# Queries and keys loaded as rows of four tokens, a new attention order, and slot inputs divided while they are copied

## The chip, the cores and the metric

The kernel runs on one core of a Trainium2 chip. A core has TensorE for matrix products (PE in the rows), VectorE (DVE), ScalarE (ACT), GpSimd (POOL) and SyncE (SP), which here only issues transfers; 16 DMA engines move data between the chip's memory (HBM) and the core's on-chip memory (SBUF). Matrix products land in PSUM, eight banks of 512 float32 in each of 128 partitions. Each engine works through its own list of instructions in order and waits on semaphores.

The metric is the device time of one execution in microseconds (us), the median of several.

## The reference, cut to what matters

```
q, k, v: 4 batches x 12 heads x 448 tokens x 64        (float32)
scores = q @ k.T / 8, causal mask; attn = exp(scores - rowmax)
attn   = attn / (attn.sum + 1e-9);  x = attn @ v       -> 1792 x 768

logits = x @ phi                                       # 1792 x 32 slots
d = exp(logits - logits.max over tokens);  d /= d.sum over tokens + 1e-9
slot_input = d.T @ x                                   # 32 x 768
slot_out[e] = relu(slot_input[e] @ w1[e]) @ w2[e]      # 8 experts of 4 slots
c = exp(logits - logits.max over slots);   c /= c.sum + 1e-9
x = c @ slot_out                                       # 1792 x 768

out = (sigmoid(x @ w_gate) * (x @ w_val)) @ w_out      # 768 -> 1536 -> 768
```

## The kernel before, in words

The kernel has three stages, and each starts on what the one before leaves.

**Attention with the slot logits.** A pair is two heads of one batch (24 pairs, number i), a group is four heads (12 groups, number g, two pairs each). For a group, `load_qk` and `load_v` bring q, k and v into `qkbuf[g % 2]` and `vbuf[g % 2]`: 128 tokens on the partitions, four chunks of tokens (the last has 64), the heads side by side; `load` issues one transfer a chunk for all four heads. Group 0 is loaded by `load_first` in two halves, heads 0 and 1 first, the keys of that half issued by ACT and all else by SP. For the split of q and k into float16 halves the group's mean square is needed first: `first_squares` and `squares_1` (groups 0 and 1, on DVE and ACT), `squares` and `add_up` (later groups, on POOL), then `spread` (a small product, psq) and `scales` (four small DVE instructions, the last ones qkp, qks and sc).

A pair then runs: `st_T` transposes its q and its k on TensorE (four transposes each into one psT bank), `st_hi` on ACT writes the scaled float16 value, `st_lo` on DVE what is left of it (both into tile qT), `score` forms the scores by three products of halves (psS; one set for each 128 queries, sets 0 to 2 and the last 64 as set 3), `st_m` masks and takes the row minimum of the negated scores on DVE, `st_e` takes the exponent on ACT into P, `st_P` transposes P on TensorE (psP), `st_C` copies it to PT on ACT or DVE, `st_V` multiplies by v (psV), `st_xu` copies, `st_Xa` transposes back (psX), `st_xn` divides by the row sums. For two pairs at once `st_Y` forms the logits (psY), `st_U` transposes them (psU). Each batch ends with the `tl_` functions: column maximum, exponents (en), and `tl_A`/`tl_a`, which gather the slots' unnormalised input over tokens in acc.

**The end of attention.** Only 32 token classes by 32 slots have been kept apart, so `fo` puts the four parts of the running maximum and sum together in eight steps on PE, DVE and ACT: `fw` is a factor for each row, `zw` the weighted sum, `fo(6)` adds the sums up (psm3), `fo(7)` takes the reciprocal `rz` and makes `fww` from fold, fw and rz. `to_slots` multiplies acc by `fww` (p4, in the rows psm with 32 columns), a copy brings it to `slotT`, and `first_inner` forms the first expert's first product (psh). Between these stand products of ones that nothing reads (`keep_warm`, psf).

**The order of the attention.** All of this is put in order by `Plan.play`: every step is an `op` with an engine and a cost, what it depends on, the buffers it takes and the time it is due; play builds the instruction lists by earliest start and due time. The table `SHIFT` and the constants `ASLACK`, `AMARGIN`, `AWAIT` move due times, so they alone decide the order of otherwise equal work. Loads are steps of an engine "D", which is SP's queue. Ten weight transfers of 1.5 MB (`load_w`) are spread over this stage.

**The experts and the gated unit.** The other expert weights and those of the gated unit follow on SP's queue into buffers that lie where the attention's tiles lay, and into the first ten again; a transfer is issued when the last reader of the buffer is done. TensorE multiplies as they come (psh, so). The gated unit at the end (psg, psv, pso, six column blocks) has a plan of its own, which the change leaves alone.

All instructions of both plans carry the number of one helper line, L218, in the rows.

## Time and profile before

| | |
|---|---|
| median of 3 runs | 528.49 us (527.89 to 530.23) |
| the profiled execution | 528.25 us, its span 526.5 us |
| TensorE busy | 480.0 us (91% of the span) |
| DVE, ACT, POOL busy | 395.3, 332.1, 279.8 us |
| moved by DMA | 101.56 MB; of 87660 packets 68784 under 512 B |
| the chain that ended last | PE 76%, DMA 12%, DVE 7% |

How the rows below are read: a timeline row has the start of the first instruction, the time to the end of the last one, the engine (q behind it means that it issues a transfer; PEld is TensorE's load of weights), the line, the operation, output<-inputs with shapes, the count, and in brackets how long the engine stood idle before it and what ended that. The ends of TensorE's instructions overlap the next one, so the step from one start to the next is the price of a product there, not the length of a row. A row of stretches has its limits, its length, and for each engine the busy time and the count in brackets, then the granted TensorE clock (1.00 is 2.4 GHz, 0.50 is 1.2 GHz), the DMA engines' mean busy share and GB/s. The chain of waits is followed back from the last instruction.

### The profile page before, as it was taken

Reading aid. Unit: us, or ns where it says so; the run is one execution under the profiler, and the core shown is the slowest. Engines: PE = TensorE matmul, PEld = TensorE weight load, DVE = VectorE, ACT = ScalarE, POOL = GpSimd, SP = SyncE. Lnnn points to the kernel's source line nnn. Section 1 sums busy time; section 2 is a strip of 40 time slices with the busy share of each in tenths; the row PEclk is TensorE's granted clock in tenths of the full one; section 3 lists DMA queues with packets and bytes.
Section 4 is the critical chain, followed back from the end, with each engine's and each line's share of the span. In section 5 each row is a group of like instructions: output and inputs, shape, how many; then the busy total and the mean of one; then the engine's idle time right before and its main releaser. Section 6 shows DMA issues by size and latency. Waiting matters only on the chain.

```text
span 526.5 us, 12472 instructions
## 1 busy us (share of the span) xinstructions
PE 480.0 (91%) x4649; PEld 295.9 (56%) x4649; DVE 395.3 (75%) x980; ACT 332.1 (63%) x740; POOL 279.8 (53%) x376
## 2 busy tenths in 40 slices
PE   5799999999999999999835579999999999989997
PEld 3467767767667676555412235555555555555553
DVE  4688989889889986521064069899999998986874
ACT  3688887889788886111190059878777588474420
POOL 4078868778768712000000013359899798867630
PEclk9899999999999999999979899999999999999999
DMA  5756646665767357799999992452063060210144
GB/s 133 170 167 196 198 106 187 139 194 178 211 162 196 126 183 273 287 423 418 408 408 425 411 395 93 164 195 90 33 241 121 0 240 2 71 51 1 60 175 184
DMA packets 87660, 101.56 MB, mean 193 GB/s; under 512 B 68784, under 2 KB 69040, under 8 KB 85552
## 3 DMA queue, kind: packets, MB, share of 16 engines
q1 hardware_dynamic: 86640, 100.55, 55.9%
q8 instruction: 36, 0.59, 0.4%
q10 hardware_dynamic: 960, 0.23, 0.2%
q14 instruction: 24, 0.20, 0.1%
HBM read 95.26 MB, written 5.51 MB: 191 GB/s over the span
## 4 chain that ended last, share of the span: by engine, by line
PE 76%; DMA 12%; DVE 7%; SPq 2%; issue 2%; ACT 1%; DVEq 0%; ACTq 0%
PE pso L218 27%; PE psP L218 9%; PE psV L218 9%; PE psS L218 8%; DMA w<-in_moe_w_dram 6%; DMA w<-in_moe_w_gate_dram 5%; PE psg L218 4%; PE psT L218 4%; PE so L1011 3%; PE psY L218 2%; PE psX L218 2%; DVE w L218 2%; SPq L218 2%; PE psh L998 2%; DMA k<-in_k_dram 1%
## 5 line engine op out<-in xcount | busy, mean ns | idle before, releaser
L218 POOL TENSOR_TENSOR hlo<-hs,hhi 128x448 f16<-128x448 f32 x48 | 69.8, 1469 | 124.7 <-ACT hhi L218 116.3
L218 PEld LDWEIGHTS <-hhi 128*128 128x128 f16 (+1 forms) x768 | 65.1, 101 | 56.0 <-issue 16.6
L218 PE MATMUL pso<-wh,hhi 128*128 128x384 f16 (+1 forms) x384 | 84.4, 328 | 4.9 <-DVE oacc L218 3.1
L218 ACT ACTIVATE P<-psS,nm 128x256 f32<-128x256 f32 (+3 forms) x168 | 82.3, 505 | 10.4 <-DVE nm L218 9.3
L218 POOL TENSOR_TENSOR oacc<-oacc,ev 128x384 f32<-128x384 f32 x56 | 76.3, 1382 | 15.9 <-ACT ev L218 15.9
L218 PE MATMUL pso<-wh,hlo 128*128 128x384 f16 (+1 forms) x384 | 82.3, 326 | 0.0
L218 PE MATMUL pso<-wl,hhi 128*128 128x384 f16 (+1 forms) x384 | 82.2, 326 | 0.0
L218 DVE CUSTOM_DVE_ANT_0 psS<-psS,cmaskq,sc 128x128 f32<-128x128 f32 (+2 forms) x144 | 62.7, 488 | 3.5 <-PE psS L218 3.3
L218 DVE SCALAR_TENSOR_TENSOR w<-w 128x1536 int32<-128x1536 int32 x30 | 62.0, 2069 | 2.4 <-ACT w L218 2.3
L218 DVE SCALAR_TENSOR_TENSOR oacc<-pso,osc,oacc 128x384 f32<-128x384 f32 x84 | 49.8, 610 | 14.0 <-PE pso L218 12.9
L218 PE MATMUL psP<-ident,P 128*128 128x128 f32 x384 | 57.6, 285 | 0.5 <-ACT P L218 0.5
L218 PE MATMUL psS<-qT,qT 64*64 64x256 f16 (+3 forms) x1008 | 50.3, 298 | 5.3 <-ACT qT L218 1.9
L218 POOL TENSOR_TENSOR sq<-sq 128x512 bf16<-128x512 bf16 (+1 forms) x80 | 51.2, 640 | 6.0
L218 ACT COPY PT<-psP 128x512 f32<-128x512 f32 x86 | 47.0, 589 | 7.0 <-PE psV L218 4.3
L218 ACT ACTIVATE w<-w 128x1536 int32<-128x1536 uint16 (+1 forms) x30 | 49.1, 1649 | 3.5 <-DMA w<-in_moe_w_gate_dram 3.5
L218 ACT ACTIVATE ev<-pso,osc 128x384 f32<-128x384 f32 x56 | 32.5, 582 | 27.7 <-PE pso L218 19.8
L218 PEld LDWEIGHTS psP<-ident,P 128*128 128x128 f32 x384 | 43.0, 144 | 7.9 <-issue 3.1
L218 PE MATMUL psV<-PT,v 128*64 128x448 f32 (+3 forms) x384 | 46.8, 385 | 0.0
L218 PEld LDWEIGHTS <-hlo 128*128 128x128 f16 (+1 forms) x384 | 33.8, 101 | 20.8
L301 DVE TENSOR_SCALAR hm<-psh,emask 128x256 f32<-128x256 f32 x8 | 5.3, 667 | 46.3 <-PE psh L998 43.8
L218 PEld LDWEIGHTS <-qT 64*64 64x64 f16 x1008 | 28.3, 109 | 20.9 <-issue 7.8
L218 PEld LDWEIGHTS psV<-PT,v 128*64 128x64 f32 x384 | 25.5, 136 | 22.8 <-issue 14.6
(298 smaller groups left out, 839.1 us busy)
## 6 DMA issues: line engine op xcount, KB each, us to landing
w<-in_moe_w_dram SPq DMA_DIRECT2D x32, 1536.0 KB, 8.4
w<-in_moe_w_out_dram SPq DMA_DIRECT2D x6, 1536.0 KB, 9.8
w<-in_moe_w_val_dram SPq DMA_DIRECT2D x6, 1536.0 KB, 13.4
w<-in_moe_w_gate_dram SPq DMA_DIRECT2D x6, 1536.0 KB, 6.6
out_dram<-oacc SPq DMA_DIRECT2D x13, 384.0 KB, 2.3
v<-in_v_dram SPq DMA_DIRECT2D x36, 128.0 KB, 3.0
q<-in_q_dram SPq DMA_DIRECT2D x33, 128.0 KB, 3.0
k<-in_k_dram SPq DMA_DIRECT2D x33, 128.0 KB, 3.0
```

Of the source, the lines that this page charges most:

```text
L218: x = f(*a, **kw)
L301: nc.vector.tensor_scalar(to.rearrange("s (i q) -> s q i", i=2), ps.rearrange("s (q i) -> s q i", i=2), 0.0, emask[:, e:e + 1], ALU.max, A ...
L998: nc.tensor.matmul(ps[32 * g:32 * g + 32, :], lhsT=slotT[:, kc, :], rhs=w[:, kc % 3, 256 * g:256 * g + 256], start=kc == 0, stop=kc == KC - 1)
L1011: nc.tensor.matmul(so[32 * c:32 * c + 32, :], lhsT=hT[:, i, 32 * g:32 * g + 32], rhs=w[:, f % 4, 256 * c:256 * c + 256], start=e == 0 and ...
```

## The change

**Rows of four tokens.** q and k of a head are read as 112 rows of four consecutive tokens: token 4p + j goes to partition p, place j. One transfer brings one head (112 partitions, four pieces of 64 values). `st_T` makes four transposes of 112 columns in place of 128, with a 112 by 112 identity. PSUM then holds the tokens by j first; `st_hi` and `st_lo` read it with a step of 112 floats (`in_order`) and write qT in token order. The squares and their sums use 112 partitions, those of group 0 go to the tile `sqbuf` in place of the second v buffer, and the four clearings of q and k tails fall away. v is loaded as before. Group 0's first half needs two transfers each of q and k in place of four.

**Division at the copy.** `fo(5)` makes `fww` from fold and fw alone. `fo(6)` forms the sums for all 128 partitions by 32 slots, `fo(7)` takes the reciprocal of that, and `to_slotT` multiplies by it while it copies to `slotT`. `to_slots` depends on `fo(5)` and no longer on `fo(7)`.

**Order.** The costs of loads in the plan are those of issuing them, with the flight as a lag; `SHIFT` and the three constants have new values; the tiles of scales and of the first squares count as buffers (`sg`, `sq`). The products that nothing reads are half as wide (256 columns), 28 in place of 19.

```
-    ASLACK, AMARGIN, AWAIT = 0.635, 1.671, 0.074
+    ASLACK, AMARGIN, AWAIT = 1.317, 1.41, 0.087
...
-    SHIFT = {('A', 0): 7.76, ('A', 1): -7.71, ('C', 0): -17.75, ('C', 1): 76.61, ('C', 2): 23.02, ('C', 3): 22.6,
+    SHIFT = {('A', 0): 8.92, ('A', 1): 24.1, ('C', 0): 11.69, ('C', 1): 67.2, ('C', 2): 31.78, ('C', 3): 30.98, ('S',
...
+        def rows_in(e, t, src):
+            for h in range(src.shape[0]):
+                e.dma_start(out=t[:RP, :, h * D:h * D + D], in_=src[h].rearrange("(p j) d -> p j d", j=RJ))
+
         def load_qk(g, w):
+            b, h0, nh = GRP[g]
             grp.setdefault(g, {"qk": qkbuf[g % 2]})
-            load(qkbuf[g % 2][w], (q, k)[w], g)
+            rows_in(sp, qkbuf[g % 2][w], (q, k)[w][b, h0:h0 + nh])
...
             for w, src in enumerate((q, k)):
-                for j, (s0, n) in enumerate(CH):
-                    (ac if w and not o else sp).dma_start(
-                        out=qkbuf[0][w][:n, j, o * D:(o + 2) * D].rearrange("p (h d) -> p h d", d=D),
-                        in_=src[0, o:o + 2, s0:s0 + n, :].rearrange("h p d -> p h d"))
+                rows_in(ac if w and not o else sp, qkbuf[0][w][:, :, o * D:(o + 2) * D], src[0, o:o + 2])
...
-            for j in range(4):
-                te.transpose(ps[:, 128 * j:128 * j + 128], grp[g]["qk"][w][:, j, o * D:(o + 2) * D], ident)
+            for j in range(RJ):
+                te.transpose(ps[:, RP * j:RP * j + RP], grp[g]["qk"][w][:RP, j, o * D:(o + 2) * D], ident[:RP, :RP])
+
+        def in_order(x):
+            return x.rearrange("p (j c) -> p c j", j=RJ)
+
+        def by_rows(x):
+            return x.rearrange("p (c j) -> p c j", j=RJ)
...
-            ac.activation(out=hi, in_=pr[i]["ps", w][:, :S], func=AF.Copy, scale=scale_of(i)[:, w:w + 1])
+            ac.activation(out=by_rows(hi), in_=in_order(pr[i]["ps", w][:, :S]), func=AF.Copy, scale=scale_of(i)[:, w:w + 1])
...
-            ve.scalar_tensor_tensor(lo, d.pop(("ps", w))[:, :S], scale_of(i)[:, w:w + 1], d["hi", w], ALU.mult, ALU.subtract)
+            ve.scalar_tensor_tensor(by_rows(lo), in_order(d.pop(("ps", w))[:, :S]), scale_of(i)[:, w:w + 1], by_rows(d["hi", w]), ALU.mult, ALU.subtract)
...
-            te.matmul(fin["f"].rearrange("p (a b) -> p a b", a=4), lhsT=ones, rhs=ones.rearrange("p (a b) -> p a b", a=1).to_broadcast([128, 4, 128]),
-                      start=True, stop=True)
+            te.matmul(fin["f"][:, :256].rearrange("p (a b) -> p a b", a=2), lhsT=ones,
+                      rhs=ones.rearrange("p (a b) -> p a b", a=1).to_broadcast([128, 2, 128]), start=True, stop=True)
...
                 ve.tensor_tensor(fin["zw"], zrun, fin["w"], ALU.mult)
+                fw = fin["fw"] = tl_p.tile([128, NS], F32, tag="mrow", name="fww")
+                ve.tensor_scalar(fw, fold, fin["w"], None, ALU.mult)
             elif n == 6:
-                fin["p3"] = psS.tile([128, 1], F32, tag="s", name="psm3")
-                te.matmul(fin["p3"], lhsT=fold4.rearrange("p a s -> p (a s)"), rhs=fin["zw"], start=True, stop=True)
+                fin["p3"] = psS.tile([128, NS], F32, tag="s", name="psm3")
+                te.matmul(fin["p3"], lhsT=fin["zw"].to_broadcast([128, 128]), rhs=fold, start=True, stop=True)
             else:
-                rz = sm_p.tile([128, 1], F32, tag="rz", name="rz")
-                ve.tensor_scalar(rz, fin["p3"], 1e-9, None, ALU.add)
+                rz = fin["rz"] = tl_p.tile([128, 1, NS], F32, tag="rz", name="rz")
+                ve.tensor_scalar(rz[:, 0], fin["p3"], 1e-9, None, ALU.add)
                 ve.reciprocal(rz, rz)
-                fw = fin["fw"] = tl_p.tile([128, NS], F32, tag="mrow", name="fww")
-                ve.tensor_scalar(fw, fold, fin["w"], rz, ALU.mult, ALU.mult)
+
+        def to_slotT(n):
+            ve.tensor_tensor(slotT[:, 3 * n:3 * n + 3], fin["p4", n], fin["rz"].to_broadcast([128, 3, NS]), ALU.mult)
...
-                    op(("p4", n), plain(to_slots, n), {"P": 0.68}, [("fo", 7), ("a", b, n)], new=[("s", ("p4", n))], due=t0 + 6.0 + n)
+                    op(("p4", n), plain(to_slots, n), {"P": 0.6}, [("fo", 5), ("a", b, n)], new=[("s", ("p4", n))], due=t0 + 6.0 + n)
```

**Three places where the order differs.** First, SP at the start. q_91 and k_95 are the buffers of the even groups (group 0 first), q_111 and k_115 those of the odd ones (group 1 first), v_123 and v_167 the values of groups 0 and 1. Before, behind group 0's first half and the second half of its q:

```order
L218 DMA k_95<-in_k_dram 128x2x64 x3
L218 DMA k_95<-in_k_dram 64x2x64
L218 DMA v_123<-in_v_dram 128x4x64 x3
L218 DMA v_123<-in_v_dram 64x4x64
L218 DMA v_167<-in_v_dram 128x4x64 x3
L218 DMA v_167<-in_v_dram 64x4x64
L218 DMA q_111<-in_q_dram 128x4x64 x3
L218 DMA q_111<-in_q_dram 64x4x64
L218 DMA k_115<-in_k_dram 128x4x64 x3
L218 DMA k_115<-in_k_dram 64x4x64
```

SP now:

```order
L220 DMA q_91<-in_q_dram 112x4x64 x4
L220 DMA k_95<-in_k_dram 112x4x64 x2
L220 DMA q_111<-in_q_dram 112x4x64 x4
L220 DMA k_115<-in_k_dram 112x4x64 x4
L220 DMA phis<-in_moe_phi_dram 64x6x32 x2
L220 DMA v_123<-in_v_dram 128x4x64 x3
L220 DMA v_123<-in_v_dram 64x4x64
L220 DMA k_95<-in_k_dram 112x4x64 x4
```

Group 1's q and k have moved from behind 20 transfers of SP to behind six, ahead of the values of both groups.

Second, TensorE in a pair in the middle, from the last scores of set 2 (psS 64x384) on; psY are the logits, psq the sums of squares of a later group, P_137 and P_138 the exponents of set 1. Before:

```order
L218 MATMUL psS<-qT_131,qT_127 64x384
L218 MATMUL psY<-xu_201,phis 64x448
L218 MATMUL psY<-xu_202,phis 64x448
L218 LDWEIGHTS avgb
L218 MATMUL psq<-sqr,avgb 128x64
L218 MATMUL psP<-ident,P_137 128x128 x2
L218 MATMUL psP<-ident,P_138 128x128 x2
```

The place of psY now, in three of the groups, later in the pair:

```order
L220 MATMUL psP<-ident,P_141 128x128 x4
L220 MATMUL psT<-ident,k_95 128x112 x4
L220 MATMUL psT<-ident,q_91 128x112 x4
L220 MATMUL psY<-xu_201,phis 64x448
L220 MATMUL psY<-xu_202,phis 64x448
L220 MATMUL psP<-ident,P_139 128x128 x2
L220 MATMUL psP<-ident,P_140 128x128 x2
L220 MATMUL psV<-PT,v_167 64x448 x2
```

The logits stand between transposes there, and no longer right behind the scores; the transposes of q and k are 112 columns wide.

Third, DVE at the end of attention, from the factors on (psm_4018 is psm3, psm_4030 and psm_4034 are p4). Before:

```order
L218 TENSOR_TENSOR zw<-zrun,fw 128x1
L218 SCALAR_TENSOR_TENSOR acc<-acc,al,psA 128x384 x2
L218 TENSOR_SCALAR rz<-psm_4018 128x1
L218 RECIPROCAL rz<-rz 128x1
L218 TENSOR_SCALAR fww<-fold,fw,rz 128x32
L218 COPY slotT<-psm_4030 128x96
L218 COPY slotT<-psm_4034 128x96
```

DVE now (psm_4015 is psm3, psm_4018 and psm_4025 are p4):

```order
L220 TENSOR_TENSOR zw<-zrun,fw 128x1
L220 TENSOR_SCALAR fww<-fold,fw 128x32
L220 SCALAR_TENSOR_TENSOR acc<-acc,al,psA 128x384 x2
L220 TENSOR_SCALAR rz<-psm_4015 128x32
L220 RECIPROCAL rz<-rz 128x32
L220 TENSOR_TENSOR slotT<-psm_4018,rz 128x96
L220 TENSOR_TENSOR slotT<-psm_4025,rz 128x96
```

The factor that the slot products read is made before acc and no longer behind the reciprocal.

## Rows read from the trace of the kernel before

**Rows 1.** Stretches: a part of attention, a part of the experts, one start-up microsecond.

```profile
60.00:80.00 20.00, 20.00 (x275) 14.23 (x273) 17.82 (x63) 17.92 (x55) 14.74 (x29) 1.00 0.45 126
240.00:260.00 20.00, 18.69 (x270) 10.93 (x272) 2.04 (x5) 2.19 (x5) 0.00 (x0) 1.00 1.02 419
22.00:23.00 1.00, 1.00 (x10) 0.71 (x5) 0.61 (x3) 0.64 (x3) 0.43 (x2) 0.50 0.69 155
```

**Rows 2.** Chain of waits, the experts' stage (start, length, what).

```profile
245.86 25.21 DMA w<-in_moe_w_gate_dram
```

**Rows 3.** SP's queue after attention (timeline).

```profile
221.52 1.64 SPq L218 DMA_DIRECT2D w<-in_moe_w_dram  x2
```

**Rows 4.** SP's queue at the start (timeline), and a load's flight (DMA issues).

```profile
0.73 4.53 SPq L218 DMA_DIRECT2D q<-in_q_dram  x8
7.62 4.77 SPq L218 DMA_DIRECT2D v<-in_v_dram  x8
14.84 2.36 SPq L218 DMA_DIRECT2D k<-in_k_dram  x4
...
q<-in_q_dram SPq DMA_DIRECT2D x33, 128.0 KB, 3.0
```

**Rows 5.** Timeline of the start, 17 to 31 us.

```profile
17.54 1.23 DVE L218 CUSTOM_DVE_ANT_0 sq<-q 128x1024 bf16<-128x1024 f32 x1 [2.48 <-DMA q<-in_q_dram]
...
19.42 0.54 PE L218 MATMUL psS<-qT,qT 64*64 64x448 f16 x3 [1.50 <-DVE qT L218]
19.75 1.06 ACT L218 ACTIVATE sq<-k 128x1024 bf16<-128x1024 f32 x1 [3.06 <-DMA k<-in_k_dram]
...
21.51 0.85 PE L218 MATMUL psS<-qT,qT 64*64 64x384 f16 x11 [1.55 <-ACT P L218]
...
22.34 1.95 PE L218 MATMUL psP<-ident,P 128*128 128x128 f32 x8
...
30.27 1.09 PE L218 MATMUL psP<-ident,P 128*128 128x128 f32 x8
```

**Rows 6.** Timeline of a pair in the middle, 96 to 101 us.

```profile
96.39 0.66 PE L218 MATMUL psP<-ident,P 128*128 128x128 f32 x4
...
96.88 0.60 PE L218 MATMUL psT<-ident,k 128*128 128x128 f32 x4
...
97.52 1.16 ACT L218 ACTIVATE qT<-psT,qks 128x448 f16<-128x448 f32 x2 [0.40 <-PE psT L218]
...
97.76 0.60 PE L218 MATMUL psP<-ident,P 128*128 128x128 f32 x4
...
98.24 1.27 DVE L218 SCALAR_TENSOR_TENSOR qT<-psT,qks,qT 128x448 f16<-128x448 f32 x2
...
98.29 1.95 PE L218 MATMUL psV<-PT,v 128*64 128x448 f32 x16
...
100.17 1.24 PE L218 MATMUL psS<-qT,qT 64*64 64x448 f16 x18
```

**Rows 7.** Timeline of the end of attention, 211 to 223 us.

```profile
211.19 0.46 PE L218 MATMUL psU<-ident,yt 64*128 64x64 f32 x4
...
214.22 0.28 DVE L218 TENSOR_REDUCE mrow<-psm 1x32 f32<-1x128 f32 x1 [0.30 <-PE psm L218]
...
216.58 1.27 DVE L218 SCALAR_TENSOR_TENSOR acc<-acc,al,psA 128x384 f32<-128x384 f32 x2 [0.78 <-PE psA L218]
...
218.15 0.30 DVE L218 TENSOR_SCALAR fww<-fold,fw,rz 128x32 f32<-128x32 f32 x1
...
218.50 1.52 PE L218 MATMUL psm<-fww,acc 128*128 128x32 f32 x12
219.96 2.80 PE L218 MATMUL psh<-w,slotT 128*32 128x256 f32 x48
...
222.83 0.66 DVE L301 TENSOR_SCALAR hm<-psh,emask 128x256 f32<-128x256 f32 x1 [2.50 <-PE psh L218]
```

**Rows 8.** The page's costliest groups: DVE's evictions at the end (busy, mean ns, idle before).

```profile
L218 DVE SCALAR_TENSOR_TENSOR oacc<-pso,osc,oacc 128x384 f32<-128x384 f32 x84 | 49.8, 610 | 14.0 <-PE pso L218 12.9
```

More of the change, by code (lines that the diff above doesn't have):

```diff
@@ L147 @@
     HG = 4
+    RJ = 4
+    RP = S // RJ
     UC = 256
@@ L367 @@
         rbuf = [sm_p.tile([128, 8], F32, name=f"r{i}") for i in range(3)]
-        for t in qkbuf[0] + qkbuf[1] + vbuf:
+        for t in vbuf:
             nc.gpsimd.memset(t[64:, 3], 0.0)
@@ L745, in group @@
             if g == 0:
-                for o, t in ((0, 4.6), (2, 2.3)):
-                    op(("ld", 0, o), lambda e: None, {"D": t}, [("ld", 0, 0)] if o else [], due=0.0,
+                for o, t in ((0, 1.2), (2, 2.2)):
+                    op(("ld", 0, o), lambda e: None, {"D": t}, [("ld", 0, 0)] if o else [], due=0.0, lag=2.6,
                        new=[] if o else [("q", ("q", 0)), ("k", ("k", 0))])
                     for w in range(2):
-                        op(("am", o, w), plain(first_squares, o, w), {"VA"[w]: 0.65}, [("ld", 0, o)])
+                        first = not o and not w
+                        op(("am", o, w), plain(first_squares, o, w), {"VA"[w]: 0.65}, [("ld", 0, o)], new=[("sq", ("sq", 0))] if first else [],
+                           use=[] if first else [("sq", 0)], behind=[] if first else [("am", 0, 0)])
                     op(("am16", o), plain(first_cast, 0, o), {"V": 0.17}, [("am", o, 0), ("am", o, 1)])
                     op(("psq", 0, o), plain(spread, 0, o), {"P": 0.1}, [("am16", o)], new=[("x", ("psq", 0, o))])
-                    op(("sc", 0, o), plain(scales, 0, o), {"V": 0.75}, [("psq", 0, o)], use=[("psq", 0, o)])
+                    op(("sc", 0, o), plain(scales, 0, o), {"V": 0.75}, [("psq", 0, o)], use=[("psq", 0, o)], new=[("sg", ("sg", 0, o))])
                 op(("phi",), lambda e: [sp.dma_start(out=phis[64 * h:64 * h + 64, :, h, :],
@@ L758, in group @@
                 for w in range(2):
-                    op(("ld", g, w), plain(load_qk, g, w), {"D": 1.7}, lag=2.0, behind=[("ld", 0, 2)], new=[("qk"[w], ("qk"[w], g))])
+                    op(("ld", g, w), plain(load_qk, g, w), {"D": 2.2}, lag=2.6, behind=[("ld", 0, 2)], new=[("qk"[w], ("qk"[w], g))])
                 for w in range(2) if g == 1 else ():
@@ L782, in pair @@
             got = ("sc", 0, o) if g == 0 else ("sc", g)
+            sg = ("sg", 0, o) if g == 0 else ("sg", g, 0)
             for w in range(2):
@@ L799, in pair @@
                     first = t == 1 and h == 0
-                    op(("m", i, t, h), plain(st_m, i, t, h), {"V": cm}, [("S", i, x) for x in ((0, 1) if t in (0, 1) else (t,))], lag=0.05, use=[bank] + ([] if first else [("nm", i)]),
+                    op(("m", i, t, h), plain(st_m, i, t, h), {"V": cm}, [("S", i, x) for x in ((0, 1) if t in (0, 1) else (t,))], lag=0.05, use=[bank, sg] + ([] if first else [("nm", i)]),
                        new=[("nm", ("nm", i))] if first else [])
@@ L875, in tail @@
                 k = 0
-                for x, m in ((("Y", i, "z"), 3), (("U", i, "z"), 5), (("psl", b), 5), (("pse", b), 2), (("A", b, 0), 1), (("A", b, 1), 3)):
+                for x, m in ((("Y", i, "z"), 5), (("U", i, "z"), 8), (("psl", b), 7), (("pse", b), 2), (("A", b, 0), 3), (("A", b, 1), 3)):
                     for n in range(m):
-                        op(("fl", k), plain(keep_warm, k), {"P": 0.22}, [x], new=[] if k else [("p", ("fl",))], use=[("fl",)] if k else [], behind=[("fl", k - 1)] if k else [],
+                        op(("fl", k), plain(keep_warm, k), {"P": 0.11}, [x], new=[] if k else [("p", ("fl",))], use=[("fl",)] if k else [], behind=[("fl", k - 1)] if k else [],
                            due=t0 + 8.0)
```

46 lines of the change are left out of this document (23 added, 23 removed), and 24 rows, old and new, of the table SHIFT.

## The prediction

> **What bounds the kernel now.** I read the stretches first, then the chain of waits, then the timeline where one of them changes hands. In the middle of attention TensorE is busy for all of 20 us while DVE and ACT reach 17.8 and 17.9 us [rows 1]; the steps from one start to the next there are those of products that follow each other without a gap [rows 6], so this stage lasts as long as the list of TensorE's products. In the experts' stage the DMA engines are full at 419 GB/s [rows 1], and the chain runs through weight transfers there [rows 2]. The reader is to see the hinge between the two: two weight transfers are issued at 221.52 us, when the psh that began at 219.96 has read its buffers [rows 3, 7], and the rest of the stream follows from there. The bytes behind it don't change, and the gated unit's plan doesn't either. So every microsecond by which psh starts earlier comes off the end, and nothing else in the change does. The sum is made for that start, 219.96 us.
>
> **The start.** Group 1's squares need its q and k, whose last transfers are issued from 14.84 to 17.2 us, behind eight transfers of v that took 4.77 us of the queue [rows 4]. DVE stands idle 2.48 us and ACT 3.06 us for them, with everything behind them in their lists waiting too: the low half of pair 1's q on DVE, for which TensorE idles 1.50 us, then pair 0's exponents on ACT, for which it idles 1.55 us [rows 5]. In the new order group 1's loads stand behind six transfers of SP. At 0.57 us a transfer (4.53 over 8) the last of its 14 is issued by 0.73 + 14 x 0.57 = 8.7 us and lands, with 3.0 us of flight [rows 4], by 11.7 us, well before either engine comes to it. So both idles go; the longer, ACT's 3.06 us, is the one that the second wait of TensorE hangs on. One of the two squares also moves to a place where ACT was idle, ahead of pair 0's exponents. Against it: the second half of group 0 is now squared by ACT ahead of the first conversions, so the first pair gets no gain from its earlier data, and pair 0's exponents stand behind one conversion (0.58 us, half of 1.16 [rows 6]). I take 3.06 - 0.58 = 2.5 us.
>
> The clock comes on top. At 22 to 23 us the granted clock is 0.50, the lower level of 1.2 GHz [rows 1], after TensorE had been idle twice for 1.5 us; eight psP transposes take 1.95 us there and 1.09 us at the higher level [rows 5]. If the two idles go, this work should stand at 2.4 GHz: 0.86 us for these eight, and some 0.5 us for the products around them, 1.3 us together. Sum of the start: -3.8 us. Bounds: -2.0 (ACT's list is the next to be late and the clock stays low) and -4.9 (all of 3.06 and 1.8 of clock).
>
> **Transposes of 112 columns.** Eight psT take 97.76 - 96.88 = 0.88 us from start to start, 109 to 110 ns each [rows 6]. The trace has no width of 112. With 64 columns four psU take 0.46 us to the end of the last; the last of four psT-like ones at 128 columns adds 0.27 us to three steps of 109 (0.60), so with some 0.23 us for the last a step at 64 is (0.46 - 0.23)/3 = 77 ns [rows 6, 7]. On a line through the two, 112 columns cost 101 ns, 8 ns less; in proportion to columns it would be 95 ns, 14 ns less. There are 24 x 8 = 192: between 1.6 and 2.6 us. Since the first step of such a row holds a change of kind, the line is too flat; I take -2.1 us. The lower bound is nothing at all, if the load of 128 stationary columns sets the step.
>
> **The order in the middle.** A change between kinds of product costs: psP to psT after scores is 0.49 us for four and psP to psV is 0.53, against 0.44 without a change [rows 6], so 0.05 to leave scores or values and 0.09 to enter them. Where psY has moved from behind the scores to between transposes, one leaving and one entering are added. I count 139 changes in the old list up to psh and 147 in the new one. Eight at 0.05 to 0.12: 0.4 to 1.0 us; I take +0.8. Apart from that the list is the same products, and it can't gain, since it had no gaps. It can lose, by a wait: see the rivals. On DVE and ACT one copy or two change sides, which is less than the 10% that both have free [rows 1]. Loads of later groups are two to four transfers of 0.57 us earlier or later on SP, hidden behind TensorE's list, in whose middle no gap ends on a load [rows 1]; without that cover each is 0.6 us.
>
> **The end of attention.** Before, the slot products (psm x12, start 218.50) wait for fww, which ends at 218.45 behind the reciprocal, though acc's first half is there at 216.58 + 0.64 = 217.22 and its second at 217.85 [rows 7]. Now fww is made ahead of acc (0.30 us that DVE has while psA runs: it idles 0.78 us there [rows 7]). The first six products start at about 217.3, the other six at 217.95 and take 0.76 us, to 218.7; psh follows at once, as it does now (219.96, the end of psm being 220.02). On the other side the copy must wait for rz: two instructions on 32 columns behind acc, 0.2 us each, 218.25, then the copy of 0.3, 218.55, and some 0.2 to the product that reads it. So psh starts at about 218.75 in place of 219.96: 1.2 us earlier. Narrower filler products ahead of psA may give 0.2 to 0.3 more. I take -1.4 us; bounds -0.8 (rz is slower on a wide operand from PSUM) and -1.9.
>
> **Reading PSUM with a step.** The two conversions of a pair and the two low halves now read every 112th float. Elements, partitions and instructions are the same. The nearest rows: acc reads psA with a step of three floats, 0.64 us for 384 elements, and the evictions read 384 in a row in 0.61 us [rows 7, 8]; mrow reads 128 elements of one partition with a step of 32 floats in 0.28 us [rows 7]. By these it is free, and I take nothing. The other way points hm, which takes 0.66 us for 256 elements and writes SBUF with a jump at every element [rows 7]. By that price it would cost a great deal: second rival.
>
> [...]
>
> **Sum.** -3.8 - 2.1 + 0.8 - 1.4 = -6.5 us. Span 526.5 - 6.5 = 520.0; the profiled execution lies 1.75 us above its span: 521.75; the median of the runs lies 0.24 above that execution: 522.0 us.
>
> **The rivals.**
>
> First, the narrow transposes bring nothing, the load being the limit (+2.1), and the end gives little, since the transfers already queued ahead of 221.52 have to land first (+1.0). For it: the stationary operand keeps its 128 columns. Against: psU with 64 columns has as many stationary ones and is faster [rows 7]. 522.0 + 2.1 + 1.0 = 525.1 us.
>
> Second, the slower one: reading with a large step costs what hm shows. 0.66/256 is 2.6 ns an element; a low half of 448 elements would go from 0.64 to 1.15 us, and a conversion on ACT perhaps from 0.58 to 1.1. The place is the chain psT, two conversions, two low halves, psS in every pair. The low halves end at 98.24 + 1.27 = 99.51 and the scores that need them start at 100.17 [rows 6]: 0.66 us of slack, so it decides from about 0.2 us for each of the instructions. Three of the four lie one behind the other, 1.5 us, which exceeds the slack by 0.85 us; a part of that is taken back by what else TensorE has. 24 pairs x 0.6 = 14 us: 522.0 + 14 = 536 us. For it: hm. Against: acc and mrow, both from PSUM. [...]
>
> Third, the new order runs dry somewhere. psU now stands closer behind psY in some pairs, and psX comes sooner behind psV; both need a copy of some 0.6 us first. 0.2 us in each of 24 pairs: +4.8, 526.8 us. For it: both copies share engines that are 90% busy [rows 1]. Against: psX still has the scores between it and psV.
>
> Fourth, everything at its better bound, -4.9 - 2.6 + 0.4 - 1.9 = -9.0, 2.5 us better than the forecast: 519.5 us.
>
> **How the numbers follow.** Forecast 0.62; first rival 0.16; third 0.09; second 0.07; fourth 0.06. The forecast's own spread is 520 to 524.5. The range takes in the first rival and the fourth and ends short of the third: 518.5 to 526.0 us, with about 0.82 in it. A measurement of this kernel can tell 0.5%, 2.6 us, from no change: below 525.85 is faster, above 531.1 slower. Forecast, first and fourth rival are faster, 0.84; the third is within the bound, 0.09; the second slower, 0.07.
>
> **What would show it.** The start: no idle of ACT or DVE for q or k beyond 12 us, no idle of TensorE above 1 us between 16 and 26 us, the clock at 1.00 in every stretch from 19 us on, the eight psP of 30.27 us at about 26.5. Transposes: eight psT in 0.78 us. Middle: TensorE without idle from 27 to 195 us. Strided reads: conversions still 0.58 and low halves still 0.64 us. End: psm x12 in two parts, the first ahead of rz, and psh at about 213.5 us. Then the transfers behind psh at about 215 and a full stream of the same length. The prediction is wrong if the conversions are longer, if gaps appear in TensorE's middle, or if the stream of weights starts earlier and its end doesn't.

## The result and the profile after

The changed kernel takes **523.69 us** (median of 7 runs, 521.18 to 525.36) against 527.58 us before (7 runs, 527.06 to 530.23): a ratio of 0.9916, 95% interval 0.9896 to 0.9936. The forecast was 522.0 us with a range of 518.5 to 526.0, so the kernel is faster as said, but by 3.9 us (0.8%) where the sum said 6.5. That the time is nearer to the forecast than the gain is luck: the kernel before came out 0.9 us lower in seven runs than in the three from which the forecast was counted. The profiled execution has a span of 522.8 us, 3.7 less than before.

Three marks divide the way to the end: the first scores of pair 2 (the start is over), the last product of values (pair 23), and psh, the first product on the experts' weights. All are starts on TensorE, in us:

| | before | after | difference |
|---|---|---|---|
| first scores of pair 0 | 8.53 | 9.73 | +1.20 |
| first scores of pair 2 | 29.09 | 26.28 | -2.81 |
| last values (length from the mark above) | 206.90 (177.81) | 203.89 (177.61) | -3.01 |
| psh (length from the mark above) | 219.96 (13.06) | 215.46 (11.57) | -4.50 |
| fourth landing of weights behind psh | 240.47 | 236.78 | -3.69 |
| span | 526.5 | 522.8 | -3.7 |

So of the 6.5 us that were to be gained by the start of psh, 4.5 came; 1.0 is missing from the start, and the middle, which was to gain 1.3, gained 0.2.

**The start.** The timeline of the changed kernel from 0 to 24 us (start, length, engine, line, operation, out<-in, count, and in brackets the idle time before it with its releaser):

```profile
0.73 2.96 SPq L220 DMA_DIRECT2D q<-in_q_dram  x4
...
5.79 0.98 PE L220 MATMUL psT<-ident,q 112*128 112x112 f32 x4 [5.79 <-DMA q<-in_q_dram]
...
7.91 0.63 ACT L220 ACTIVATE sq<-k 112x512 bf16<-112x512 f32 x1 [2.02 <-DMA k<-in_k_dram]
8.54 1.14 ACT L220 ACTIVATE qT<-psT,qks 128x448 f16<-128x448 f32 x2
...
10.37 1.06 ACT L220 ACTIVATE sq<-q 112x1024 bf16<-112x1024 f32 x1 [0.69 <-DMA q<-in_q_dram]
...
14.88 1.12 PE L220 MATMUL psP<-ident,P 128*128 128x128 f32 x4 [1.34 <-ACT P L220]
16.64 1.22 DVE L220 CUSTOM_DVE_ANT_0 sq<-k 112x1024 bf16<-112x1024 f32 x1
20.18 0.68 PE L220 MATMUL psS<-qT,qT 64*64 64x384 f16 x11 [0.62 <-ACT P L220]
20.83 1.07 PE L220 MATMUL psP<-ident,P 128*128 128x128 f32 x8
```

Against [rows 5]: the idles of 2.48 and 3.06 us for group 1 are gone (0.69 us and none), TensorE's waits of 1.50 and 1.55 us have become one of 1.34 at pair 0's exponents and one of 0.62, and the eight psP take 1.07 us in place of 1.95. What is new stands at the top: a transfer of 112 x 4 x 64 holds SP for 0.74 us (2.96 for four), and the first data are used at 5.79 us. ACT then waits 2.02 us for pair 1's k ahead of pair 0's conversions, which begin at 8.54 us.

**The clock** in the stretch from 22 to 23 us is at 1.00, the upper level, where it was 0.50 [rows 1] (columns: stretch, length, busy time of PE, PEld, DVE, ACT, POOL, granted clock, DMA share, GB/s):

```profile
22.00:23.00 1.00, 1.00 (x29) 0.91 (x22) 0.57 (x6) 1.00 (x4) 0.00 (x0) 1.00 0.79 176
```

**The middle.** Eight psT followed by psP take 30.79 - 30.02 = 0.77 us, 96 ns each, against 109 to 110 [rows 6]:

```profile
30.02 0.55 PE L220 MATMUL psT<-ident,k 112*128 112x112 f32 x4
30.41 0.55 PE L220 MATMUL psT<-ident,q 112*128 112x112 f32 x4
...
30.79 0.60 PE L220 MATMUL psP<-ident,P 128*128 128x128 f32 x4
```

168 of the 192 transposes lie between the first two marks; at 13 ns each that would be 2.2 us. This stretch, the list of TensorE in what follows, became only 0.2 us shorter (177.81 to 177.61). The waits of TensorE between 26 and 205 us show where the rest went (us in total, times, longest); before, this view had no row at all in the same stretch:

```profile
PE psq L220 <- POOL sqr L220: 1.4, 3, 0.8
PE psl L220 <- POOL ln L220: 0.2, 1, 0.2
```

psq is the small product on a group's sums of squares, which GpSimd adds up from the third group on. Its first wait, TensorE and GpSimd in the changed kernel:

```profile
35.28 0.66 PE L220 MATMUL psP<-ident,P 128*128 128x128 f32 x4
36.69 0.19 PE L220 MATMUL psq<-sqr,avgb 112*128 112x64 bf16 x1 [0.75 <-POOL sqr L220]
```

```profile
25.51 2.04 POOL L220 TENSOR_TENSOR sq<-q 112x512 bf16<-112x512 f32 x2 [4.24 <-DMA q<-in_q_dram]
27.63 2.80 POOL L220 TENSOR_TENSOR sq<-sq 112x512 bf16<-112x512 bf16 x4
...
31.41 2.04 POOL L220 TENSOR_TENSOR sq<-k 112x512 bf16<-112x512 f32 x2
33.52 2.79 POOL L220 TENSOR_TENSOR sq<-sq 112x512 bf16<-112x512 bf16 x4
36.39 0.24 POOL L220 TENSOR_TENSOR sqr<-sq 112x32 bf16<-112x32 bf16 x1
```

From start to start these four psP take 1.41 us; without a wait 0.49. Counted in this way, against the same rows without a wait, the places are 35.3 (0.91 us), 98.3 (0.48), 119.1 (0.27, the psl, which waits for GpSimd's ln) and 159.3 (0.37): 2.0 us. GpSimd stands idle for 4.24 us until the third group's q lands, although its k landed 5.5 us earlier (19.73 against 25.19).

**The end.** After the last values (11.57 us to psh in place of 13.06 [rows 7]):

```profile
212.65 0.24 DVE L220 TENSOR_SCALAR fww<-fold,fw 128x32 f32<-128x32 f32 x1
213.27 1.27 DVE L220 SCALAR_TENSOR_TENSOR acc<-acc,al,psA 128x384 f32<-128x384 f32 x2 [0.39 <-PE psA L220]
...
214.03 1.50 PE L220 MATMUL psm<-fww,acc 128*128 128x32 f32 x12
...
214.67 0.35 DVE L220 RECIPROCAL rz<-rz 128x32 f32<-128x32 f32 x1
215.13 0.26 DVE L220 TENSOR_TENSOR slotT<-psm,rz 128x96 f32<-128x96 f32 x1
...
215.46 2.80 PE L220 MATMUL psh<-w,slotT 128*32 128x256 f32 x48
```

fww no longer stands behind the reciprocal, and psm begins at 214.03, 0.76 us behind the start of acc (1.92 before [rows 7]). rz and the copy lie beside psm, and psh follows 1.43 us behind its start (1.46 before).

### The profile page after: what moved, and what is told of

It reads as the page before. It is cut to its first block, busy times and chain, and to the rows that moved or that the text cites. A ratio compares the mean times of both kernels' runs of the same rounds, so it can differ in the third digit from the quotient of the medians.

```text
span 522.8 us, 12445 instructions
## 1 busy us (share of the span) xinstructions
PE 475.4 (91%) x4658; PEld 294.5 (56%) x4658; DVE 393.6 (75%) x980; ACT 330.0 (63%) x740; POOL 278.4 (53%) x372
## 4 chain that ended last, share of the span: by engine, by line
PE 71%; DMA 11%; DVE 7%; POOL 5%; issue 2%; ACT 2%; SPq 1%; DVEq 0%; POOLq 0%; ACTq 0%
PE pso L220 26%; PE psP L220 7%; PE psS L220 7%; PE psV L220 6%; DMA w<-in_moe_w_dram 5%; POOL sq L220 5%; PE so L1027 4%; PE psg L220 4%; PE psh L1014 3%; PE psT L220 3%; DMA q<-in_q_dram 2%; DVE w L220 2%; PE psY L220 2%; DMA w<-in_moe_w_out_dram 2%; PE psX L220 2%
## 5 line engine op out<-in xcount | busy, mean ns | idle before, releaser
L220 ACT ACTIVATE P<-psS,nm 128x384 f32<-128x384 f32 (+3 forms) x168 | 82.3, 506 | 11.8 <-DVE nm L220 9.5
L220 PE MATMUL psP<-ident,P 128*128 128x128 f32 x384 | 59.4, 282 | 1.3 <-ACT P L220 1.3
L220 POOL TENSOR_TENSOR sq<-sq 112x512 bf16<-112x512 bf16 (+1 forms) x80 | 51.2, 641 | 6.0
L220 ACT ACTIVATE ev<-pso,osc 128x384 f32<-128x384 f32 x56 | 32.6, 584 | 28.0 <-PE pso L220 20.3
L220 PE MATMUL psS<-qT,qT 64*64 64x256 f16 (+3 forms) x1008 | 48.7, 294 | 1.3 <-ACT P L220 0.6
L1022 ACT COPY hT<-psht 128x256 f32<-128x256 f32 x8 | 3.0, 373 | 56.6 <-PE psht L1020 49.8
```

Of the source, the lines that this page charges most:

```text
L220: x = f(*a, **kw)
L1022: nc.scalar.copy(hT, pt)
```

## The experiments

They ask four things: what the rows of four are worth without the new order; what the end is worth by itself; whether the waits for sums are what the middle lost; and what holds the start. All times are set against runs of the kernel before on the same chip (527.5 us).

### The rows of four in the old order

The kernel before with the new load, 112-column transposes and stepped reads; of the edit, the transposes:

```diff
-            for j in range(4):
-                te.transpose(ps[:, 128 * j:128 * j + 128], grp[g]["qk"][w][:, j, o * D:(o + 2) * D], ident)
+            for j in range(RJ):
+                te.transpose(ps[:, RP * j:RP * j + RP], grp[g]["qk"][w][:RP, j, o * D:(o + 2) * D], ident[:RP, :RP])
```

> The kernel before, in its own order, with q and k in rows of four, transposes of 112 columns and the stepped reads; no new order, old end. Theory (the gain at the start comes from fewer transfers ahead of group 1's loads, and eight psT cost 0.77 instead of 0.88 us): SP reaches group 1's k some 3 us sooner, so the idles of 2.48 and 3.06 us shrink, first scores come about 0.6 us later than 8.53, the list between pair 2's first scores and pair 23's values shrinks from 177.8 to about 175.3 us, and psh starts at about 215 to 216; time about 524. Rival (the new order is what gives the start): the idles stay, only the transposes count, psh at about 217.5 us and time about 525.5. Rival (stepped reads cost in this order): conversions longer than 0.58 us, list longer than 177.8.

528.47 us, ratio 1.0011 (0.9993 to 1.003): nothing gained. The theory and both rivals missed. First scores came at 9.58 us, pair 2's at 27.93 (1.2 us earlier than before), but the list took 179.06 us, 1.25 longer, and psh began at 220.03. SP began on group 1's k at 14.44 us, only 0.4 sooner in place of 3: the eight transfers of v ahead of it took 6.68 us here and 4.77 before [rows 4], and ACT still idled 2.39 us for k. The list is longer, but the reads aren't: the medians of conversions and low halves are 634 and 678 ns, against 635 and 677 before. TensorE's waits in its middle:

```profile
PE psq L220 <- POOL sqr L220: 2.7, 2, 2.0
PE psT L220 <- ACT P L220: 0.4, 1, 0.4
```

So here too the faster transposes ended in a wait for sums of squares.

### GpSimd takes k first

The changed kernel; in `squares` and in `add_up`:

```diff
+            i = 1 - i
```

> The changed kernel, with GpSimd squaring and adding up k ahead of q in every group from the third on (k lands 2.5 to 5.5 us sooner); everything else in its place. Theory (the three waits of TensorE for sums of squares, 0.9, 0.5 and 0.4 us, come from GpSimd idling 2.8 to 4.2 us for q): they go, the list between pair 2's scores and pair 23's values shrinks from 177.6 to about 176.0 us, psh starts at about 213.9, and 1.0 to 1.5 us of that comes off the end: about 522.4 against 523.7. Rival (GpSimd's own 10 us of work for a group set the time, or its sums r, which stand in between): the waits shrink by less than half, psh later than 214.8, no difference in time.

522.35 us (6 runs), ratio 0.9882 (0.986 to 0.9904). The list fell to 175.61 us, psh began at 213.59, and TensorE's one wait left between 26 and 205 us is another:

```profile
PE psY L220 <- ACT xu L220: 0.2, 1, 0.2
```

The same place on GpSimd, which now begins 4.0 us sooner and has its sums at 32.6, 3.3 us ahead of the psq of 35.90:

```profile
21.49 2.04 POOL L220 TENSOR_TENSOR sq<-k 112x512 bf16<-112x512 f32 x2
...
27.38 2.04 POOL L220 TENSOR_TENSOR sq<-q 112x512 bf16<-112x512 f32 x2
...
32.37 0.25 POOL L220 TENSOR_TENSOR sqr<-sq 112x32 bf16<-112x32 bf16 x1
```

This shows the cause of the loss in the middle: 2.0 us of the list, by two lines that change no product, no load and no order on any engine but GpSimd. It isn't chance between executions either: the four profiled kernels with k first and 112 columns in the new order have lists of 175.57 to 175.64 us, the three without these lines 177.53 to 178.67.

### The same in the old order, twice

rows_alone with the two lines, for all groups:

> The kernel of rows_alone (order and end of before, q and k in rows of four) with GpSimd adding up k ahead of q. Theory (rows_alone gained nothing only because TensorE waited 2.07 and 0.74 us for sums of squares that come late when q lands 0.8 us later and TensorE's list is shorter): both waits go, the list from pair 2's scores to pair 23's values falls from 179.06 to about 176.3 us, psh starts at about 217.3 in place of 220.03, and time is 2 to 3 us lower, about 526.0. Rival (the old order itself holds the list up, whoever comes first on GpSimd): list above 178 us and no difference in time from 528.5.

529.94 us, ratio 1.0051 (1.0033 to 1.0069): a miss, and slower. The two waits went, and a larger one came (GpSimd, TensorE, and then two stretches, columns as above):

```profile
60.21 2.04 POOL L220 TENSOR_TENSOR sq<-k 112x512 bf16<-112x512 f32 x2 [8.32 <-DMA k<-in_k_dram]
...
73.39 0.21 PE L220 MATMUL psq<-sqr,avgb 112*128 112x64 bf16 x1 [3.62 <-POOL sqr L220]
```

```profile
74.00:78.00 4.00, 4.00 (x23) 3.67 (x25) 1.42 (x8) 2.31 (x6) 1.01 (x3) 0.50 0.13 28
78.00:80.00 2.00, 2.00 (x34) 1.73 (x31) 1.47 (x6) 0.34 (x1) 1.92 (x4) 0.72 0.00 0
```

This wait cost more than its own length. The list took 183.75 us, 8.0 more than in the next kernel, and behind the wait TensorE's granted clock stood at 0.50, its lower level of 1.2 GHz, for 4 us; the wait of 2.0 us in rows_alone had left it at 1.00.

In the old order the fifth and sixth groups issue q ahead of k, which I had not looked up. With k first in all but these two:

```diff
+            i = i if g in (4, 5) else 1 - i
```

> The kernel of rows_alone, with GpSimd adding up k first in the groups whose k is issued first, and q first in the two (the fifth and the sixth, as before) whose q is. In rows_keys k came first in those two as well, and TensorE waited 4.9 us in one place for it. Theory: with the sums in the order of landing no wait of TensorE for sums is over 0.5 us, the list from pair 2's scores to pair 23's values is 176.0 to 176.5 us (177.81 before), psh starts at about 217.2 in place of 220.0, time about 525.7 against 528.5: the rows of four are worth some 2 us in the old order as well, once the sums are not late. Rival (the old order holds the list up elsewhere too): list above 178 us, no gain.

525.08 us, ratio 0.9952 (0.9935 to 0.9968); list 175.74 us, psh at 217.47, no wait over 0.5 us in the middle. So the rows of four are worth 2.1 us of list in the old order as well, if the sums are ready. And the list is as long as that of keys_first in the new order (175.61): the new order is worth 0.1 us in the middle. What it brings lies at the start, where this kernel reaches pair 2's scores only at 28.68 us (26.40 in keys_first). Part of that is the clock. rows_alone has the same start and came to this mark at 27.93; TensorE had idled 1.70 us there and 1.74 here for pair 0's exponents, but the stretch behind it ran at 1.00 in rows_alone and at 0.53 here (first rows_alone, then this kernel):

```profile
23.00:26.00 3.00, 3.00 (x46) 2.53 (x44) 2.48 (x15) 2.81 (x9) 0.00 (x0) 1.00 0.98 200
```

```profile
23.00:26.00 3.00, 3.00 (x36) 2.59 (x35) 1.68 (x13) 1.69 (x6) 1.85 (x2) 0.53 0.65 144
```

So this idle time is followed by the lower clock in some executions and not in others.

### Transposes of 128 columns

```diff
-                te.transpose(ps[:, RP * j:RP * j + RP], grp[g]["qk"][w][:RP, j, o * D:(o + 2) * D], ident[:RP, :RP])
+                te.transpose(ps[:, RP * j:RP * j + 128], grp[g]["qk"][w][:, j, o * D:(o + 2) * D], ident)
```

> The kernel of keys_first with transposes of 128 columns in place of 112 (the 16 added columns are zeros that the next transpose writes over), same order. Theory (the step of a transpose goes with its columns): eight psT take 0.88 us from start to start in place of 0.77, the list from pair 2's scores to pair 23's values is 168 x 13 ns = 2.2 us longer than 175.61, psh 2.4 us later than 213.59, at about 216.0. Rival (the 128 stationary columns set the step, and the faster transposes of the changed kernel come from their place in the order): list within 0.5 us of 175.6.

One execution, 528.57 us; the time and psh (220.21) say nothing, since the zeros in the added columns had to be written ahead of the first loads, and SP issued its first at 4.51 us. The list says it: 177.80 us, 2.19 longer than 175.61. Eight psT at 128 columns:

```profile
98.41 0.60 PE L220 MATMUL psT<-ident,k 128*128 128x128 f32 x4
98.84 0.60 PE L220 MATMUL psT<-ident,q 128*128 128x128 f32 x4
99.28 0.60 PE L220 MATMUL psP<-ident,P 128*128 128x128 f32 x4
```

99.28 - 98.41 = 0.87 us against 0.77. So the 128 stationary columns, which all of these kernels have, don't set the step. The edit widens the transposes and also makes them read 128 partitions in place of 112; the two weren't tried apart.

### Reads without a step

```diff
-            ac.activation(out=by_rows(hi), in_=in_order(pr[i]["ps", w][:, :S]), ...
+            ac.activation(out=hi, in_=pr[i]["ps", w][:, :S], ...
```

and the same for the low half. This kernel leaves the tokens in the order of the transposes, so it doesn't compute the reference; it is there for its times.

> The kernel of keys_first with conversions and low halves that read PSUM and write SBUF without a step (448 floats in a row), so that the tokens stay in the order in which the transposes leave them. Theory (a step of 112 floats in PSUM and of four in SBUF costs nothing): two conversions 1.14 to 1.19 us and two low halves 1.27 to 1.28 us, as in the changed kernel, and the list from pair 2's scores to pair 23's values within 0.2 us of 175.6. Rival (the step costs something, hidden where these engines wait): low halves or conversions shorter by 0.05 us or more each.

One execution, 522.40 us; list 175.59 us. The medians of the 48 conversions and 48 low halves, first keys_first (with a step), then this kernel (count, min/median/max in ns, first and last start):

```profile
L220 ACT ACTIVATE qT<-psT,qks x48: 616/634/662, 8.7 to 190.3; 128x448 f16<-128x448 f32 x48
L220 DVE SCALAR_TENSOR_TENSOR qT<-psT,qks,qT x48: 667/676/686, 9.3 to 191.3; 128x448 f16<-128x448 f32 x48
```

```profile
L220 ACT ACTIVATE qT<-psT,qks x48: 613/634/662, 8.7 to 190.4; 128x448 f16<-128x448 f32 x48
L220 DVE SCALAR_TENSOR_TENSOR qT<-psT,qks,qT x48: 669/676/684, 9.4 to 191.4; 128x448 f16<-128x448 f32 x48
```

The step costs nothing, to the nanosecond of the medians.

### The end alone

The kernel before with the division at the copy, and without the four fillers between psA (the product that acc is formed from) and psh:

```diff
-                rz = sm_p.tile([128, 1], F32, tag="rz", name="rz")
...
-                ve.tensor_scalar(fw, fold, fin["w"], rz, ALU.mult, ALU.mult)
+        def to_slotT(n):
+            ve.tensor_tensor(slotT[:, 3 * n:3 * n + 3], fin["p4", n], fin["rz"].to_broadcast([128, 3, NS]), ALU.mult)
```

> The kernel before with the division moved to the copy of the slots and the four filler products behind psA left out (psA to psh is then free of them); all else as before. Theory (the end gives its time back only in part, since the transfer issued at 212.95 us still lands at 221.54): psh 1.2 us earlier, at about 218.8, the landings behind it earlier by 0.3 to 0.8, time 0.3 to 0.8 lower, about 527.0. Rival A (all of it comes off the end): landings and end 1.2 us earlier, 526.4. Rival B (the clock falls without the fillers): the eight rows behind psA at the lower clock, psh no earlier, time as before.

526.71 us, ratio 0.9984 (0.9968 to 0.9999). From the last values to psh 12.28 us against 13.06: 0.78 gained, not 1.2. The start of this run was 0.4 us later, so psh and the fourth landing behind it both came 0.3 us earlier than before: all of it came through, which speaks for rival A's rule and against the theory's, at a smaller size. Rival B falls, since the clock stayed at 1.00 from 205 to 224 us. In the changed kernel, whose fillers have 256 columns in place of 512, psA begins 0.3 us sooner after the last values (8.45 against 8.73), and the remaining 0.4 of its 1.49 lies between psA and psh (3.13 against 3.55), where TensorE waits for the second copy to slotT in this kernel:

```profile
219.68 1.50 PE L218 MATMUL psh<-w,slotT 128*32 128x256 f32 x24 [0.35 <-DVE slotT L218]
```

### A later release of the weights' buffers

The row of the fourth landing shows -3.69 us where psh has -4.50. I thought that the transfer ahead of psh, which lands 1.7 us after the next is issued, holds the stream. The changed kernel, with fillers between the first four and the other psh:

```diff
+                if n == 0 and c == 0:
+                    for x in range(8):
+                        keep_warm(1)
```

> The changed kernel with eight filler products of 0.109 us, 0.87 us in all, between the first four and the other psh products, so that the two buffers come free 0.87 us later. Theory (the stream of weights behind psh is held in the changed kernel by the transfer issued before it, which lands at 218.74, 1.7 us after the next is issued; so 0.8 us of psh's earlier start is lost): the landings from the fourth transfer behind psh on don't move by more than 0.2 us against the landing of the one ahead of psh (18.0 us behind it), and the time between psh and the fourth landing grows from 21.3 to about 21.5 us only where it should grow to 22.2. Rival (every us of psh's start counts one for one): the landings move by 0.87 us against that landing, to 18.9 us behind it.

One execution, 525.14 us. The release came 1.44 us later than in the changed kernel (218.47 against 217.03; this run's start was 0.3 us late too), the landing ahead of psh 0.99 later (219.73), the fourth landing behind it 0.23 (237.01). By the theory's own measure it held: the fourth landing is 17.3 us behind the landing ahead of psh, not 18.9. But it came 18.5 us behind the release, as in ten other kernels here (18.7 to 19.3), and 19.75 is what the changed kernel has. So the later release didn't cost; the changed kernel's run had 0.8 us too much. late_half (below) has it as well (19.8), keys_first with the same code there doesn't (19.0). The theory isn't borne out, and what took these 0.8 us in two of the profiled executions is open.

### The start

The changed kernel with ACT's square of pair 1's k behind pair 0's conversions:

```diff
+            if o and w and not later:
+                later.append((first_squares, (o, w)))
+                return
...
```

> The changed kernel, with ACT's squares of k for pair 1, and what hangs on them, behind the two conversions of pair 0 instead of ahead of them. Theory (of the 1.2 us by which the first scores come later than before, 9.73 against 8.53 us, half is this square on ACT and half the later landing of the first transfers): conversions start at about 8.05 instead of 8.54, first scores at about 9.2, pair 2's scores at 25.8 instead of 26.28, psh 0.5 us earlier; time 0.3 to 0.5 us lower, hardly to be told from none by the runs. Rival (something else is late next at the start, such as the squares of group 1): first scores earlier, pair 2's scores not.

523.62 us, ratio 0.9924 (0.9903 to 0.9946): no difference, and the first scores at 9.71 as before the edit. In this run the first q was used at 6.04 us instead of 5.79; counted from there the scores are 0.27 us sooner, half of what was expected, since conversions then wait for the scales from DVE (2.04 us idle on ACT, ended by qks at 8.50). So the square wasn't the only limit, and the data were the other: see the last two kernels. The profiled execution was the slowest of the six and lost 1.1 us of list as well (178.67), with waits for sums of 2.2 us in total, so its psh at 216.75 doesn't measure the edit.

Pair 0 in the chunks of before, on top of keys_first:

```diff
+                for j, (s0, n) in enumerate(CH):
+                    (ac if w else sp).dma_start(
+                        out=qkbuf[0][w][:n, j, :2 * D].rearrange("p (h d) -> p h d", d=D),
+                        in_=src[0, :2, s0:s0 + n, :].rearrange("h p d -> p h d"))
...
```

> The kernel of keys_first with pair 0's q and k in the chunks of before (transfers of 128 x 2 x 64, transposes of 128 columns, plain reads), the rest in rows of four. Theory (the first scores come late because a transfer of 112 x 4 x 64 takes 0.7 us to issue and 3.6 to 4.2 us to land, so pair 0's q is there at 5.7 instead of 5.1 us): first q at 5.1, first scores at about 9.2 instead of 9.7 to 9.9, psh 0.4 to 0.6 us earlier than 213.59; time about 521.9, hardly to be told from keys_first by the runs. Rival (the second half's square of k on ACT, which waits for a transfer issued 0.4 us later now, holds the conversions): first scores not before 9.7, psh within 0.2 us.

521.17 us (4 runs), ratio 0.9877 (0.9858 to 0.9896): not to be told from keys_first. The rival holds: the first square began at 5.3 and the scales were ready at 7.2 us, but ACT waited for pair 1's k, and first scores came at 10.53:

```profile
8.71 0.63 ACT L220 ACTIVATE sq<-k 112x512 bf16<-112x512 f32 x1 [2.57 <-DMA k<-in_k_dram]
...
9.34 1.14 ACT L220 ACTIVATE qT<-psT,qks 128x448 f16<-128x448 f32 x2
```

Both edits together, on keys_first:

> The kernel of keys_first_pair with ACT's square of k for pair 1, and what hangs on it, behind pair 0's two conversions (as in late_half). Theory (in keys_first_pair pair 0's scales were there at 7.2 us instead of 8.1, but ACT waited 2.57 us for pair 1's k and began the conversions at 9.34): conversions begin at about 7.4, first scores at about 8.6 in place of 9.9 and 10.5, pair 2's scores at about 25.2 in place of 26.4, psh at about 212.4, time about 521.0 and below both kernels. Rival (the squares of group 1 or pair 0's exponents are late next): first scores at 8.6, pair 2's scores not before 26, no difference from keys_first.

520.62 us (5 runs, 518.75 to 521.49), ratio 0.986 (0.9835 to 0.9884): below the kernel before and, by its interval, below the changed kernel; from keys_first it can't be told by the times. Conversions began at 7.19, first scores came at 8.40 us, pair 2's at 25.68, psh at 212.89. Of 1.5 us at the first scores 0.7 is left at pair 2. ACT stands idle for group 1's q, which is now issued from 5.92 us on in place of 5.07; that this takes the rest wasn't tried by itself:

```profile
7.19 1.16 ACT L220 ACTIVATE qT<-psT,qks 128x448 f16<-128x448 f32 x2 [1.17 <-DVE qks L220]
...
11.15 1.06 ACT L220 ACTIVATE sq<-q 112x1024 bf16<-112x1024 f32 x1 [1.80 <-DMA q<-in_q_dram]
```

## Why the prediction was right in sign and short in size

Up to psh, the terms of the sum and what they measured:

| term | forecast | measured | from |
|---|---|---|---|
| start | -3.8 | -2.8 | pair 2's first scores |
| transposes | -2.1 | -2.2 | wide_keys against keys_first (list only) |
| order in the middle | +0.8 | 0 | rows_sorted against keys_first: 175.74 and 175.61 |
| waits for sums | 0 | +2.0 | keys_first against after: 175.61 and 177.61 |
| end | -1.4 | -1.5 | last values to psh |
| psh | -6.5 | -4.5 | |

**The start** was right in mechanism: the idles for group 1 went, the clock stayed at its upper level, and the eight psP came at 20.83 at that clock. The size was off by 1.0 us, and the step that failed is "the first pair gets no gain from its earlier data". There was no earlier data: I took 0.57 us of SP and 3.0 us of flight from [rows 4], but the first transfers of 112 x 4 x 64 took 0.74 us each and landed after 3.4 to 3.7 us (median of the issues in that stretch) where those of 128 x 2 x 64 took 2.4 on SP and 2.9 on ACT. The last q of pair 0 was issued sooner (1.49 us for 2.23) and landed later (5.66 for 5.06). With ACT's square of pair 1's k ahead of the conversions, first scores came 1.2 us later. best, which takes both back, reaches them at 8.40. As 1.5 us at the first scores are worth 0.7 at pair 2's there, this doesn't account for all of the 1.0 us; what took the rest is open. The 1.3 us for the clock are no fixed price of such idles: rows_alone idled 1.70 us and kept its clock.

**The waits for sums** are the step that failed most: "hidden behind TensorE's list, in whose middle no gap ends on a load; without that cover each is 0.6 us". The sum had them at nothing. The list was named as the cover, but the one who needs a load there is GpSimd, and its lead, the time from a sum's end to its use, was small. Rows of the kernel before that I didn't read, TensorE's first psq and GpSimd's last sum ahead of it:

```profile
38.20 0.20 PE L218 MATMUL psq<-sqr,avgb 128*128 128x64 bf16 x1
```

```profile
26.19 2.04 POOL L218 TENSOR_TENSOR sq<-q 128x512 bf16<-128x512 f32 x2 [3.50 <-DMA q<-in_q_dram]
...
37.07 0.24 POOL L218 TENSOR_TENSOR sqr<-sq 128x32 bf16<-128x32 bf16 x1
```

The sums were there at 37.31, 0.9 us before they were needed, and GpSimd had idled 3.50 us for q in front of them. The change brings TensorE to that place at 35.78, 2.4 us sooner, and GpSimd only 0.7 sooner. The difference of the two is 1.7, less the lead of 0.9: 0.8 us of wait, and 0.75 is in the row. The lead could have been read beforehand, and among the ten groups it went down to 0.4 us (a sum ready at 165.98, used at 166.34); how far GpSimd would move needed an estimate. The third rival (the order runs dry) had the sign right, but its mechanism, copies ahead of psU and psX, didn't occur, nor did its 4.8 us; it was sized on the wrong engine.

**Transposes** were right: 0.77 us for eight against a forecast of 0.78. From the kernel before to rows_sorted, too, the 168 psT fall from 19.1 to 17.0 us from start to start. The first rival's half "narrow transposes bring nothing" fell with wide_keys.

**The order's changes of kind** cost nothing that shows: the 0.4 to 1.0 us that I counted at 0.05 to 0.12 a change isn't there. It moves between rows: between the first two marks the 360 psP take 45.2 us in keys_first and 43.6 in rows_sorted, the 92 psX 10.1 and 11.8.

**The stepped reads** cost nothing, as said; the second rival falls with plain_reads. ACT's conversions and DVE's low halves take 634 and 676 ns with a step of 112 floats, 634 and 676 without. The Trainium skill ("SBUF — State Buffer", section "Door 1: The DMA port swizzle") says that any access pattern in PSUM that isn't contiguous significantly slows down matmuls. It says so of matmuls, and these are reads by ACT and DVE; no run here tries it on a matmul.

**The end** was right in sum (-1.5), with a reciprocal on 32 columns of 0.35 us where I took 0.2, and 0.3 ahead of psA, which I put down to the fillers of 256 columns; that wasn't tried by itself.

**From psh to the end** I took one for one. In the profiled executions 4.5 became 3.7; no rule shows in what was lost. The changed kernel's run lost 0.8 us by the fourth landing and another 1.5 at one later landing (5.27 us behind the one ahead, where neighbours stand 3.7 apart). The run of before lost 1.7 us at its last row of products in the experts' stage: it ran at a granted clock of 0.57, which is partly the lower level of 1.2 GHz, and took 3.63 us where rows_alone needed 1.93 (before, its stretch, then rows_alone):

```profile
301.01 3.63 PE L1011 MATMUL so<-w,hT 128*32 128x256 f32 x24 [1.02 <-DMA w<-in_moe_w_dram]
...
300.00:306.00 6.00, 4.02 (x26) 1.53 (x26) 0.78 (x2) 0.00 (x0) 0.00 (x0) 0.57 1.02 400
```

```profile
301.00 1.93 PE L1021 MATMUL so<-w,hT 128*32 128x256 f32 x24 [1.76 <-DMA w<-in_moe_w_dram]
```

-4.5 + 0.8 + 1.5 - 1.7 = -3.9, and psg, the first product of the gated unit, came 3.84 us earlier. Single executions differ by such pieces of 0.8 to 1.7 us; so a term under 1 us is better read between marks inside the trace than from two spans.

## What to carry to other kernels

When an engine that was never waited for stands in front of the bounding engine's work, read its lead, not its busy share: when its result is there, when it is used, and which load it idled for; whatever makes the bounding engine faster eats that lead first. Let a helper engine take its inputs in the order in which they land. A layout that makes fewer or narrower products may make slower transfers, and at the start, where nothing hides them, the first transfers may keep the old layout.

## What was not expected of the hardware

- A transfer of 112 x 4 x 64 floats (112 KB, 256 bytes a piece) took 0.74 us of SP's queue at the start and 3.4 to 3.7 us to land, one of 128 x 2 x 64 (64 KB) about 0.5 and 2.4 to 2.9. Four tokens in a row don't make larger pieces: all 5225 packets of the changed kernel's first 9 us are under 512 bytes, 247 on average.
- The step of an fp32 transpose went with its columns: 96 ns at 112 and 109 at 128, a ratio of 0.88, while the stationary operand stayed at 128 columns. The partitions read went from 112 to 128 with them.
- From the third landing behind psh on, the weights mostly land 3.6 to 4.1 us apart. In two of the thirteen profiled executions (the changed kernel and late_half) one of these steps is 5.3 us, in plain_reads one is 4.8; what sets them apart isn't known.
- At the same place of the start, TensorE idled 1.70 us in one execution (rows_alone) and its granted clock stayed at 1.00; in another (rows_sorted) it idled 1.74 us and the clock was 0.53 from 23 to 26 us.
